# Stage 1 and the first projection of a three-stage layer in one written order, with scores on quarter tiles of TensorE

## The chip, the cores and the metric

The kernel runs on one core of one Trainium2 chip. The metric is the device time of one execution in microseconds (us). TensorE is called PE in the profile, VectorE DVE, ScalarE ACT, GpSimd POOL; SP issues the loads.

## What is computed

Three stages follow one another on a batch of 2 with 768 rows. The change touches the first stage and the first projection of the second.

```python
def _attn_ref(q, k, v):                       # 2 batches, 8 heads, 768 rows, 64 wide
    block, window = (32, 16)
    k_sum = k.reshape(B, H, nb, block, D).max(axis=3)      # 24 block keys
    v_sum = v.reshape(B, H, nb, block, D).mean(axis=3)     # 24 block values
    scores_l = scale * q @ k.T, masked to |i - j| < window
    scores_s = scale * q @ k_sum.T + log(block)
    a = softmax(concatenate([scores_l, scores_s], -1))
    return a @ concatenate([v, v_sum], 2)
def _moe_ref(x):       # 4 experts: q, k, v of 64 columns from x, causal softmax, @ v @ wo, top-2 gates
def _moe2_ref(x):      # token mixing (768 -> 256 -> 768), then channel mixing (512 -> 1536 -> 512)
```

## The kernel before, in words

Heads are taken in pairs, four to a batch. For each pair stage 1 cuts the 768 queries into 12 tiles of 64 rows, both heads of the pair stacked to 128 rows; the keys that a tile can see are a window of 96, and 24 block maxima stand behind them, 120 columns in all. Four tiles make a group (24 groups in the two batches, three to a pair).

A group goes through these steps, each named by a word in the list FIRST: S, scores on PE (`s1_scores`, L217; an f32 product takes two instructions; the query tile `qb` is spread over 128 rows with zeros for the other head, which is why `qb` is first set to zero, L634 and L635); mn, the masked minimum on DVE (`s1_minima`, L227); ex, the exps with their sums on ACT (L236); sm and ri, the inverse sums on POOL and DVE; mu, the products on POOL (L249 in batch 0, L252 in batch 1); T, four transposes on PE (L257); pT, their copy on ACT (L262); V, the product with the values on PE (L271), 64 columns at a time into one of two column halves; xh and xl, the high part by ACT (L279) and the low part by DVE (L282). Products later on are made of three terms of such high and low parts (`mm3`, L112 to L114).

Keys come as a ready window of 12 x 120 columns (`kwT`, tile `kx`), except for batch 0's first pair, which loads the plain keys (`kt`) and copies them into windows on DVE (L194 to L197). `km` (L185, L189) takes the block maxima and a copy (L187) puts them behind each window. Block means of v are made on PE in batch 0, by 12 products a pair with a matrix of zeros and 1/32 (`vm`, L293); in batch 1 by a DVE sum of a second copy of v (`vt`, L203) and a transpose (L208). POOL writes them behind the value windows (`vx`, L329, L211).

Batch 0's stage 1 stands in the written order FIRST: each engine is held to the order of the words. Batch 1's stage 1 (`s1`, one step a group) and the projection of batch 0 (`proj`, `pv` of 260 columns and `pj` of 384) are generators that `run` mixes by a share of progress, after which the planner of the framework orders the engines by its own estimate. `proj` copies q and k parts to their places by DMAs on the SP queue (L449 to L453). The SP queue issues in order: batch 0's loads, the projection weights, then batch 1's loads as the planner placed them, with the first token weights (`raw`, L140) among them. The score tiles have three PSUM banks (`sc`), transposes and block sums three (`pt`), values two (`acc`).

Of the kernel before, what the change touches and what calls it, by code (L numbers as in the profile page):

```python
# [39 lines left out]
kx0 S0 S1 mn0 ex0 S2 mn1 vm0.0 ex1 sm0 mn2 vm0.1 ri0 km1 mu0 vm0.2 ex2 kx1 sm1 T0 ri1 S3 mu1 pT0 S4  # L40
vme0 sm2 mn3 vx0 ex3 T1 ri2 mn4 S5 mu2 pT1 V0 mn5 ex4 sm3 vm1.0 ri3 km2 mu3 V1 xh0 T2 kx2 sm4 xh1 T3
xl0 ex5 vm1.1 ri4 xl1 mu4 vm1.2 pT2 sm5 S6 ri5 pT3 mu5 vme1 S7 mn6 vx1 ex6 T4 mn7 T5 S8 km3 ex7 sm6
V2 ri6 kx3 mu6 V3 mn8 xh2 S9 sm7 pT4 xl2 xh3 ri7 S10 pT5 mu7 mn9 ex8 T6 xl3 T7 V4 ex9 sm8 mn10 V5
wh0 S11 ri8 wh1 wl0 wh2 pT6 vm2.0 wl1 sm9 wh3 xh4 wl2 mu8 pT7 vm2.1 xl4 ex10 ri9 wl3 vm2.2 mn11 mu9
# [9 lines left out]
def stack_kernel(ctx: ExitStack, tc, qT, kT, kwT, vw, vT, wqkv, wo, tok1, tok2, ch1, ch2,  # L54
# [125 lines left out]

    def s1_keys(kt, vt, kx, vx):
        km = sp1.tile([P, NBLK], F32, name="km")
        sums = (kx[:, :, KW:KX], km[:, None, :].broadcast_to([P, NT, NBLK]))
        if kt is None:
            vec.tensor_reduce(km.rearrange("p (t n) -> p t n", t=NT),  # L185
                              kx[:, :, WIN:WIN + TQ].rearrange("p t (n c) -> p t n c", c=BLK), axis=AX.X, op=ALU.max)
            vec.tensor_copy(*sums)  # L187
# [12 lines left out]

    def s1_sums(kt, vt, kx, vx):
        vs = sp1.tile([P, NBLK], F32, name="vs")
        vec.tensor_reduce(vs, vt.rearrange("p (n c) -> p n c", c=BLK), axis=AX.X, op=ALU.add)  # L203
        return vs
# [586 lines left out]
```

## Time and profile before

| | us |
|---|---|
| median of 3 runs | 469.67 (468.07 to 472.20) |
| the profiled execution, whole | 467.73 |
| its span, from first to last instruction | 465.9 |
| PE, DVE, ACT, POOL busy | 445.1, 280.1, 231.2, 285.2 |

The rows below come from the one profiled execution, so sums are made against its 467.73 us. L numbers are lines of the kernel before; a line can be a helper's. Tile names in the rows are the program's, with numbers of buffers left out.

### The profile page before, as it was taken

Reading aid. Unit: us, or ns where it says so; the run is one execution under the profiler, and the core shown is the slowest. Engines: PE = TensorE matmul, PEld = TensorE weight load, DVE = VectorE, ACT = ScalarE, POOL = GpSimd, SP = SyncE. Lnnn points to the kernel's source line nnn. Section 1 sums busy time; section 2 is a strip of 40 time slices with the busy share of each in tenths; the row PEclk is TensorE's granted clock in tenths of the full one; section 3 lists DMA queues with packets and bytes.
Section 4 is the critical chain, followed back from the end, with each engine's and each line's share of the span. In section 5 each row is a group of like instructions: output and inputs, shape, how many; then the busy total and the mean of one; then the engine's idle time right before and its main releaser. Section 6 shows DMA issues by size and latency. Waiting matters only on the chain.

```text
span 465.9 us, 8565 instructions
## 1 busy us (share of the span) xinstructions
PE 445.1 (96%) x3038; PEld 420.7 (90%) x3038; DVE 280.1 (60%) x818; ACT 231.2 (50%) x653; POOL 285.2 (61%) x319
## 2 busy tenths in 40 slices
PE   7899899999989878999999999999999999999996
PEld 7798789989978766897999999999999999999996
DVE  5573766759699679868773743677572673332322
ACT  4685665977778687885664423233323321111010
POOL 4568542768989887997873869877864771000000
PEclk9999999999999999999999999999999999999999
DMA  7999917806515865021111120212121100001111
GB/s 222 275 255 310 289 39 207 182 2 167 127 46 152 210 171 146 3 91 45 45 47 46 66 70 2 84 53 78 58 91 45 62 32 0 1 0 69 68 70 68
DMA packets 28522, 46.51 MB, mean 100 GB/s; under 512 B 2496, under 2 KB 19648, under 8 KB 28480
## 3 DMA queue, kind: packets, MB, share of 16 engines
q1 hardware_dynamic: 28480, 45.97, 35.2%
q8 instruction: 24, 0.39, 0.4%
q14 instruction: 18, 0.15, 0.1%
HBM read 33.38 MB, written 3.15 MB: 78 GB/s over the span
## 4 chain that ended last, share of the span: by engine, by line
PE 68%; DMA 10%; DVE 7%; POOL 4%; ACT 3%; issue 3%; SPq 3%; DVEq 0%; ACTq 0%; POOLq 0%
PE h L113 7%; PE h L112 7%; PE h L114 7%; PE o L112 7%; PE o L113 7%; PE o L114 7%; DMA kx<-in_kwT_dram 5%; PE s1s L217 4%; PE s1a L271 2%; DMA qb<-in_qT_dram 2%; POOL pr L492 2%; PE u L112 2%; PE pj L112 2%; PE u L113 2%; PE u L114 2%
## 5 line engine op out<-in xcount | busy, mean ns | idle before, releaser
L144 POOL TENSOR_SCALAR deca<-deca 128x512 f32<-128x512 f32 x30 | 58.0, 1938 | 10.5 <-ACT deca L143 9.7
L113 PE MATMUL o<-hl,c2h 128*128 128x384 f32 x192 | 64.2, 337 | 0.0
L114 PE MATMUL o<-hh,c2l 128*128 128x384 f32 x192 | 64.0, 336 | 0.0
L108 ACT ACTIVATE hh<-h 128x384 fp32r<-128x384 f32 x48 | 23.3, 490 | 79.4 <-PE h L114 78.8
L109 DVE SCALAR_TENSOR_TENSOR hl<-h,hh 128x384 fp32r<-128x384 f32 x48 | 26.5, 555 | 53.2 <-ACT hh L108 53.2
L605 DVE TENSOR_TENSOR oa<-o,oa 128x384 f32<-128x384 f32 x64 | 31.9, 550 | 38.5 <-PE o L114 38.5
L112 PE MATMUL o<-hh,c2h 128*128 128x384 f32 x192 | 49.4, 336 | 0.0
L236 ACT ACTIVATE pr<-n,mn 128x120 f32<-128x120 f32 x96 | 36.6, 384 | 16.3 <-DVE mn L227 15.8
L150 POOL TENSOR_TENSOR raw<-raw 128x512 f32<-128x512 f32 x30 | 31.3, 1042 | 20.4 <-DVE raw L147 18.6
L492 POOL TENSOR_SCALAR pr<-pr,f,wg 128x128 f32<-128x128 f32 (+5 forms) x48 | 40.1, 849 | 5.1 <-DVE f L489 2.9
L151 POOL TENSOR_TENSOR deca<-deca,raw 128x512 f32<-128x512 f32 x30 | 40.8, 1360 | 1.0
L149 ACT ACTIVATE raw<-raw 128x512 f32<-128x512 uint32 x30 | 20.3, 677 | 36.3 <-DMA raw<-in_ch_dram 25.6
L145 DVE TENSOR_SCALAR deca<-deca 128x512 int32<-128x512 int32 x30 | 27.8, 928 | 14.9 <-POOL deca L144 14.9
L486 ACT ACTIVATE pr<-pr,mn 128x128 f32<-128x128 f32 (+5 forms) x48 | 31.9, 665 | 9.8 <-DVE mn L481 9.7
L113 PEld LDWEIGHTS o<-hl,c2h 128*128 128x128 f32 x192 | 36.0, 188 | 0.3 <-DVE hl L109 0.3
L114 PEld LDWEIGHTS o<-hh,c2l 128*128 128x128 f32 x192 | 36.0, 188 | 0.0
L112 PEld LDWEIGHTS o<-hh,c2h 128*128 128x128 f32 x192 | 34.8, 188 | 0.1
L113 PE MATMUL h<-u0l,c1h 128*128 128x384 f32 x96 | 32.5, 338 | 0.0
L112 PE MATMUL h<-u0h,c1h 128*128 128x384 f32 x96 | 32.4, 338 | 0.0
L114 PE MATMUL h<-u0h,c1l 128*128 128x384 f32 x96 | 32.3, 337 | 0.0
L112 PE MATMUL h<-u1h,c1h 128*128 128x384 f32 x96 | 32.3, 336 | 0.0
L113 PE MATMUL h<-u1l,c1h 128*128 128x384 f32 x96 | 32.3, 336 | 0.0
(207 smaller groups left out, 1315.1 us busy)
## 6 DMA issues: line engine op xcount, KB each, us to landing
raw<-in_ch_dram SPq DMA_DIRECT2D x24, 512.0 KB, 3.5
kx<-in_kwT_dram SPq DMA_DIRECT2D x7, 720.0 KB, 10.0
vx<-in_vw_dram SPq DMA_DIRECT2D x8, 576.0 KB, 11.1
qb<-in_qT_dram SPq DMA_DIRECT2D x16, 192.0 KB, 8.9
raw<-in_tok_dram SPq DMA_DIRECT2D x6, 512.0 KB, 4.6
out_dram<-oa SPq DMA_DIRECT2D x16, 192.0 KB, 2.0
vt<-in_vT_dram SPq DMA_DIRECT2D x4, 384.0 KB, 10.3
rqk<-in_wqkv_dram SPq DMA_DIRECT2D x4, 256.0 KB, 10.2
```

The lines of the kernel that those rows point to most:

```text
L109: vec.scalar_tensor_tensor(lo, src, 0.0, hi.bitcast(F32), op0=ALU.max, op1=ALU.subtract)
L112: ten.matmul(out, lh, rh, start=start, stop=False)
L113: ten.matmul(out, lh, rl, start=False, stop=False)
L114: ten.matmul(out, ll, rh, start=False, stop=stop)
L144: gps.tensor_scalar(af, af, F64_TINY, F64_HUGE, op0=ALU.max, op1=ALU.min)
L145: vec.tensor_scalar(ta, ta, 3, 0x3FFFFFFF, op0=ALU.logical_shift_left, op1=ALU.bitwise_and)
L150: gps.tensor_mul(lf, lf, ef)
L151: gps.tensor_add(af, af, lf)
L236: act.activation(pr[:, i, :], n[:, i, :], AF.Exp, bias=mn[:, i:i + 1], scale=-1.0, accum_out=sm[:, i:i + 1])
L486: act.activation(prs[r], prs[r], AF.Exp, bias=mn[:, r, ci:ci + 1], scale=-1.0, accum_out=sm[:, r:r + 1])
L492: gps.tensor_scalar(prs[r][:, :nk], prs[r][:, :nk], f[:, r:r + 1], wg[:, 3 * h + r, e:e + 1], op0=ALU.mult, op1=ALU.mult)
L605: vec.tensor_add(oa[d], a[:, :HALF], oa[d])
```

## The change

Both batches' stage 1 and the projection of batch 0 are now words of one written order (a for batch 0, b for batch 1, pv, vh, vl, pj, jh, jl and the gate's gA, gE, gB for the projection, whv0 and its like for weight splits, ld0 to ld3 for batch 1's loads). A score word u covers six tiles of a pair and writes two banks, one per head: each head and tile is a matmul of 64 rows by 64 columns of the array, at row half j and column half i % 2. Batch 0 reads the plain keys (800 columns) of every pair, loaded once, and makes 96 columns and 24 columns in two matmuls; batch 1 keeps windows of 120. Queries are loaded in one piece, without zeros. The minima, exps and products work on groups of three tile pairs (360 columns in place of 480). Batch 0's block sums of v go to four column tiles of 32, three products each; a DVE copy and one product (vs) add the four parts. Batch 0's xh is a DVE copy instead of an ACT copy. Batch 1's loads stand behind the score words that free their tiles; two of its query tiles lie in the buffers of the `raw` weights. `proj_parts` holds the steps of `proj` one by one; batch 1's projection runs through it as before.

```diff
+NU = NT // 4
+NSL = 2 * NT - 2 + 32
+KP = S + 2 * WIN
...
+akm0 aS0 amn0.0 aex0.0 amn0.1 aS1 ld0 aex0.1 avm0 amn1.0 amn1.1 aex1.0 asm0 ari0 apa0 amu0.0 akm1
+avs0 aex1.1 amu0.1 aT0.0 aS2 ame0 asm1 apT0.0 avx0 ari1 aT0.1 amn2.0 aex2.0 amn2.1 amu1.0 aS3 ld1
+amu1.1 apT0.1 aT1.0 aex2.1 amn3.0 aV0 amn3.1 aT1.1 apT1.0 axh0 asm2 avm1 apT1.1 axl0 aex3.0 aV1 ari2
+apa1 amu2.0 akm2 avs1 aex3.1 amu2.1 aT2.0 axh1 aS4 axl1 apT2.0 asm3 ari3 aT2.1 ame1 amn4.0 amu3.0
...
+bkm0 asm7 aV6 wlv3 ari7 bkc0 amu7.0 wlq1 bS0 axh6 amu7.1 aT7.0 axl6 whk1 apT7.0 aT7.1 bsu0 pv0 whk2
+apT7.1 whk3 wlk1 whq2 bmn0.0 bvs0 whq3 bex0.0 aV7 wlq2 wlq3 bS1 axh7 wlk3 vh0 axl7 pv1 bme0 bmn0.1
+bvx0 bex0.1 bkm1 pv2 vh1 bkc1 bsm0 bri0 vl1 bmu0.0 pv3 vh2 wlk2 bmu0.1 vl2 bT0.0 vh3 pv4 vl0 bpT0.0
...
+bT3.0 bxh2 bT3.1 bpT3.0 bS4 bxl2 bpT3.1 bvs3 jh2 bmn4.0 bV3 bme3 bmn4.1 bex4.0 bvx3 pj4 jl2 bxh3
+bex4.1 bxl3 bS5 jh3 bsm4 pj5 bmn5.0 jh4 bex5.0 bmn5.1 bri4 jl3 bmu4.1 bex5.1 jl4 bS6 bmu4.0 pj6 jh5
+bmn6.0 bex6.0 bmn6.1 bsm5 bri5 jl5 bmu5.0 bex6.1 pj7 bmu5.1 jh6 jl6 bsm6 bT4.0 bri6 jh7 bT4.1 bmu6.0
+bS7 bpT4.0 jl7 bpT4.1 bmu6.1 bT5.0 bmn7.0 bT5.1 bex7.0 bT6.0 bmn7.1 bV4 bex7.1 bxh4 bsm7 bri7 bpT5.0
+bxl4 bmu7.0 bpT5.1 bT6.1 bpT6.0 bV5 bmu7.1 bpT6.1 bT7.0 bxh5 bV6 bpT7.0 bxl5 bT7.1 bxh6 bpT7.1 bxl6
+bV7 bxh7 bxl7
 """
...
     def s1_load(b, hp, qb):
-        first = b == 0 and hp == 0
-        kx = unit([P, NT, KX], F32, f"kx{b}{hp}")
-        kt = None
-        if first:
-
-            kt = kt0
-            vec.memset(kx[:, 0, KW:KX], 0.0)
-
+        kx = unit([P, KP + NBLK] if b == 0 else [P, NT, KX], F32, f"kx{b}{hp}")
         vt = half([P, S], F32, "vt") if b else None
         vx = unit([P, NT, P], F32, f"vx{b}{hp}")
-        loads = [(kt, kT) if first else (kx, kwT[b, hp])]
-        loads += [(qb[i::2, :, i, :], qT[b, hp, i::2].rearrange("p (t c) -> p t c", c=P)) for i in range(2)]
-        if first:
+        loads = [(kx, kwT[hp]) if b else (kx[:, :KP], kT[hp]), (qb, qT[b, hp])]
+        if b == 0 and hp == 0:
             loads += [(lmask, lmask_d), (ident, ident_d), (blocks, blocks_d)]
-        loads += ([(vt, vT[b, hp])] if b else []) + [(vx[:KW], vw[b, hp])]
+        loads += ([(vt, vT[hp])] if b else []) + [(vx[:KW], vw[b, hp])]
         for d, src in loads:
-            if b == 0:
-                r = tc.keep_in_program_order(nc.sync.dma_start(d, src))
-            else:
-                with tc.issue_after(last["load"].ins):
-                    r = nc.sync.dma_start(d, src)
-        last["load"] = r
-        return kt, vt, kx, vx
-
-    def s1_keys(kt, vt, kx, vx):
-        km = sp1.tile([P, NBLK], F32, name="km")
-        sums = (kx[:, :, KW:KX], km[:, None, :].broadcast_to([P, NT, NBLK]))
-        if kt is None:
+            tc.keep_in_program_order(nc.sync.dma_start(d, src))
+        return kx, vt, vx
...
+    class Stage1:
...
+        def km(self, hp):
+            kx = self.lds[hp][0]
+            if self.b == 0:
+                vec.tensor_reduce(kx[:, KP:], kx[:, WIN:WIN + S].rearrange("p (n c) -> p n c", c=BLK), axis=AX.X, op=ALU.max)
+                return
+            km = self.box["km", hp] = sp1.tile([P, NBLK], F32, name="km")
...
+        def kc(self, hp):
+            vec.tensor_copy(self.lds[hp][0][:, :, KW:KX], self.box["km", hp][:, None, :].broadcast_to([P, NT, NBLK]))
...
+        def vm(self, hp):
+            pv = self.box["vm", hp] = bank("pt", f"vm{self.b}{hp}")
+            for t in range(NT):
+                c = 32 * (t % 4)
+                ten.matmul(pv[c:c + 32, P:2 * P], blocks[:KW, 2 * (NT - 1 - t):2 * (NT - 1 - t) + 32],
+                           self.lds[hp][2][:KW, t, :], start=t < 4, stop=t >= NT - 4)
...
+        def pa(self, hp):
+            parts = self.box["pa", hp] = sp1.tile([P, P], F32, name="parts", bufs=1)
+            vec.tensor_copy(parts, self.box["vm", hp][:, P:2 * P])
...
+        def vs(self, hp):
+            if self.b == 0:
+                ten.matmul(self.box["vm", hp][:NBLK, :P], blocks[:, NSL:], self.box["pa", hp], start=True, stop=True)
+                return
+            pv = self.box["vm", hp] = bank("pt", f"vm{self.b}{hp}")
+            ten.transpose(pv[:NBLK, :P], self.box["su", hp], ident)
...
+        def S(self, u):
+            qb, kx = self.qbs[u // 2], self.lds[u // 2][0]
+            sc = self.box["S", u] = [bank("sc", f"s1s{self.b}{u}{j}") for j in range(2)]
+            for part in range(1 if self.b else 2):
+                for i in range(6):
+                    t = 6 * (u % 2) + i
+                    for j in range(2):
+                        hs = slice(64 * j, 64 * j + 64)
+                        c = KX * (i // 2)
+                        if self.b:
+                            cs, k = slice(c, c + KX), kx[hs, t, :]
+                        elif part == 0:
+                            cs, k = slice(c, c + KW), kx[hs, TQ * t:TQ * t + KW]
+                        else:
+                            cs, k = slice(c + KW, c + KX), kx[hs, KP:]
+                        ten.matmul(sc[j][64 * (i % 2):64 * (i % 2) + 64, cs], qb[hs, TQ * t:TQ * t + TQ], k,
+                                   start=True, stop=True)
...
+        def mn(self, u, j):
+            n = sp1.tile([P, NU, KX], F32, name="n", bufs=3)
+            mn = sp1.tile([P, NU], F32, name="mn", bufs=6)
+            for i in range(NU):
+                t = NU * (u % 2) + i
+                mi = 0 if t == 0 else (2 if t == ST - 1 else 1)
+                vec.tensor_tensor_reduce(n[:, i, :], self.box["S", u][j][:, KX * i:KX * i + KX], lmask[:, mi, :],
+                                         scale=-0.125, scalar=BIG, op0=ALU.add, op1=ALU.min, accum_out=mn[:, i:i + 1])
+            self.box["mn", u, j] = n, mn
...
+        def xh(self, u):
+            hi, av = self.out(u, 0), self.box["V", u][:, :HALF]
+            last["x"] = vec.tensor_copy(hi, av) if self.b == 0 else act.activation(hi, av, AF.Copy)
...
-    def s1(xh, xl, qbs):
...
+    def proj_parts(b, xs, out, tags):
+        q2, k2, k2l, V = [], [], [], []
         out.extend((q2, k2, k2l, V))
-        lg = gp.tile([P, ST, NE], F32, name="lg", bufs=1)
-        for st in range(ST):
-            a = bank(next(rr), f"pv{b}{st}")
+        gate = {}
...
+        return dict(pv=pv, vh=vh, vl=vl, gA=gA, gE=gE, gB=gB, pj=pj, jh=jh, jl=jl)
...
-    qbs = []
-    for i in range(HP):
-        qb = sp1.tile([P, ST, 2, P], F32, name="qb", bufs=2) if i < 2 else unit([P, ST, 2, P], F32, f"qb{i}")
-        (vec if i < 2 else gps).memset(qb[:, :3], 0.0)
-        gps.memset(qb[:, 3:], 0.0)
-        qbs.append(qb)
+    qbs = [sp1.tile([P, S], F32, name="qb", bufs=2) for i in range(2)]
+    q0s = qbs + [half([P, S], F32, f"qb{i}") for i in range(2, HP)]
...
-    def w_split():
-        for w, r in zip(wqk, raws[1:]):
-            for k in range(HP):
-                with tc.issue_after(last["mul"].ins):
-                    split_h(w[0][:, k], r[:, k])
-                    with tc.issue_after(last["mn", 0, HP - 1, 2].ins):
-                        split_l(w[0][:, k], w[1][:, k], r[:, k], gps if k == HP - 1 else vec)
-                yield
...
+    first = Stage1(0, q0s)
     for hp in range(HP):
-        lds.append(s1_load(0, hp, qbs[hp]))
+        first.ld(hp)
...
+    second = Stage1(1, qbs + [dec.tile([P, S], F32, tag="raw", name=f"qd{i}") for i in range(2)])
     sts = [[], []]
-    g1 = s1(*xs[1], qbs[:2])
-    p0 = proj(0, *xs[0], sts[0])
-    run((12, g1), (18, part(p0, 10)), (2 * HP, w_split(), 0, 0.3))
+    p0 = proj_parts(0, first.halves, sts[0], rot(("acc", "pt", "sc")))
+    ws1 = {w: (t, r) for w, t, r in zip("vqk", (wv, *wqk), raws)}
+
+    def step(word):
+        stem = word.rstrip("0123456789.")
+        num = [int(x) for x in word[len(stem):].split(".") if x]
+        if word[:2] in ("wh", "wl"):
+            (w, r), k = ws1[word[2]], num[0]
+            if word[1] == "h":
+                split_h(w[0][:, k], r[:, k])
+            else:
+                split_l(w[0][:, k], w[1][:, k], r[:, k], gps if k == HP - 1 else vec)
+        elif stem == "ld":
+            second.ld(*num)
+        elif stem in p0:
+            p0[stem](*num)
+        else:
+            getattr((first, second)["ab".index(stem[0])], stem[1:])(*num)
+
+    in_order(FIRST.split(), step)
...
-    run((4, p0, 0, 0.2), (16, attn(0, *sts[0], yTs[0])), (14, proj(1, *xs[1], sts[1]), 0, 0.9), (8, wt_load(), 0.4, 0.8))
+    run((16, attn(0, *sts[0], yTs[0])), (14, proj(1, *xs[1], sts[1]), 0, 0.9), (8, wt_load(), 0.4, 0.8))
```

## Rows read from the trace of the kernel before

**Rows 1.** The first part of the page: busy us, share of the span, instructions.

```profile
PE 445.1 (96%) x3038; PEld 420.7 (90%) x3038; DVE 280.1 (60%) x818; ACT 231.2 (50%) x653; POOL 285.2 (61%) x319
```

**Rows 2.** Busy time by stretch: engines, then granted clock, DMA share, GB/s.

```profile
6.70:101.50 94.80, 88.22 (x946) 80.31 (x944) 57.30 (x312) 65.52 (x275) 53.69 (x111) 1.00 0.78 206
6.70:60.00 53.30, 47.67 (x524) 43.34 (x523) 30.85 (x173) 35.29 (x154) 32.80 (x59) 1.00 1.04 278
...
120.00:200.00 80.00, 72.26 (x447) 61.84 (x446) 67.13 (x197) 61.42 (x159) 71.60 (x74) 1.00 0.44 114
```

**Rows 3.** TensorE in order of time: start, us, line, operation, tiles, [idle before].

```profile
6.74 2.98 PE L217 MATMUL s1s<-kx,qb 128*128 128x120 f32 x24
...
15.93 2.12 PE L217 MATMUL s1s<-kx,qb 128*128 128x120 f32 x16 [1.20 <-DMA qb<-in_qT_dram]
...
111.45 0.33 PE L114 MATMUL pj<-x0h,wqk1l 128*128 128x384 f32 x1
```

**Rows 4.** The same view: neighbours from which distances of starts are read.

```profile
22.74 1.93 PE L293 MATMUL vm<-vx,blocks 96*24 96x128 f32 x16
...
75.51 1.09 PE L217 MATMUL s1s<-kx,qb 128*128 128x120 f32 x8
76.44 0.60 PE L257 MATMUL s1p<-ident,pr 128*120 128x128 f32 x4
76.97 0.69 PE L271 MATMUL s1a<-pTs,vx 120*64 120x64 f32 x16
77.58 0.45 PE L112 MATMUL pj<-x0h,wqk0h 128*128 128x384 f32 x1
77.87 0.34 PE L113 MATMUL pj<-x0l,wqk0h 128*128 128x384 f32 x1
78.04 0.34 PE L114 MATMUL pj<-x0h,wqk0l 128*128 128x384 f32 x1
```

**Rows 5.** TensorE groups, 0 to 112 us: count | busy, mean ns | idle before.

```profile
L217 PE MATMUL s1s<-kx,qb 128*128 128x120 f32 x192 | 27.3, 285 | 4.9 <-DVE mn L227 3.6 <-DMA qb<-in_qT_dram 1.2
L257 PE MATMUL s1p<-ident,pr 128*120 128x128 f32 x96 | 16.4, 277 | 0.0
L271 PE MATMUL s1a<-pTs,vx 120*64 120x64 f32 x384 | 15.7, 227 | 0.0
L293 PE MATMUL vm<-vx,blocks 96*24 96x128 f32 x96 | 11.4, 273 | 1.7 <-DMA vx<-in_vw_dram 1.7
```

**Rows 6.** Waits, 0 to 112 us, engines and SP queue: total, times, longest.

```profile
DVE km L185 <- DMA kx<-in_kwT_dram: 13.5, 5, 5.8
...
SPq L449 <- ACT s000h L104: 18.3, 1, 18.3
```

**Rows 7.** The SP queue in order of time: start, us, what it issued.

```profile
0.72 0.39 SPq L174 DMA_DIRECT2D kt<-in_kT_dram  x1
1.88 1.43 SPq L174 DMA_DIRECT2D qb<-in_qT_dram  x2
...
32.28 1.53 SPq L177 DMA_DIRECT2D kx<-in_kwT_dram  x1
...
74.45 0.79 SPq L177 DMA_DIRECT2D kx<-in_kwT_dram  x1
```

**Rows 8.** ACT and DVE groups, 0 to 112 us.

```profile
L279 ACT ACTIVATE x0h<-s1a 128x256 fp32r<-128x256 f32 x12 | 4.2, 368 | 0.2 <-PE s1a L271 0.2
...
L227 DVE CUSTOM_DVE_ANT_0 n<-s1s,lmask 128x120 f32<-128x120 f32 x96 | 21.4, 277 | 7.3 <-PE s1s L217 5.7 <-ACT pTs L262 1.0 <-ACT pr L236 0.5
...
L105 DVE TENSOR_TENSOR V<-pv,V 128x128 fp32r<-128x128 f32 x18 | 4.9, 283 | 2.3 <-ACT V L104 2.1
...
L105 DVE TENSOR_TENSOR s010l<-pj,s010h 128x384 fp32r<-128x384 f32 x2 | 1.1, 554 | 0.0
```

**Rows 9.** Load issues of the run: count, KB each, us to landing.

```profile
kx<-in_kwT_dram SPq DMA_DIRECT2D x7, 720.0 KB, 10.0
...
kt<-in_kT_dram SPq DMA_DIRECT2D x1, 400.0 KB, 2.9
```

More of the change, by code (lines that the diff above doesn't have):

```diff
@@ L39 @@
 FIRST = """
[L40 to L44, printed above, removed]
@@ new lines, in ri, with mu @@
+        def ri(self, u):
+            ri = self.box["ri", u] = sp1.tile([P, 2, NU], F32, name="ri", bufs=4)
+            vec.reciprocal(ri, self.box["sm", u])
+        def mu(self, u, j):
+            pr, ri = self.box["ex", u, j], self.box["ri", u]
+            if self.b == 0:
+                gps.tensor_mul(pr, pr, ri[:, j, :, None].broadcast_to([P, NU, KX]))
+                return
+            for i in range(NU):
+                gps.tensor_scalar(pr[:, i, :], pr[:, i, :], ri[:, j, i:i + 1], 1.0, op0=ALU.mult, op1=ALU.mult)
@@ new lines, in T, with pT, V @@
+        def T(self, u, j):
+            pT = self.box["T", u, j] = bank("pt", f"s1p{self.b}{u}{j}")
+            for i in range(NU):
+                ten.transpose(pT[:KX, P * i:P * i + P], self.box["ex", u, j][:, i, :], ident)
+        def pT(self, u, j):
+            pTs = self.box["pT", u, j] = sp1.tile([P, HALF], F32, name="pTs", bufs=4)
+            act.activation(pTs[:KX], self.box["T", u, j][:KX, :HALF], AF.Copy)
+        def V(self, u):
+            av = self.box["V", u] = bank("acc", f"s1a{self.b}{u}")
+            for i in range(6):
+                cs = slice(64 * i, 64 * i + 64)
+                for j in range(2):
+                    sl = slice(64 * j, 64 * j + 64)
+                    ten.matmul(av[sl, cs], self.lds[u // 2][2][:KX, 6 * (u % 2) + i, sl], self.box["pT", u, j][:KX, cs],
+                               start=True, stop=True)
@@ L336, in s1_first, with halves, in_order @@
+        def halves(self):
+            return [self.x[i][0] for i in range(2)], [self.x[i][1] for i in range(2)]
+    def in_order(words, steps):
         traced = nc.cur_bb.bb.instructions
-        for word in FIRST.split():
+        for word in words:
             at = len(traced)
-            op = word.rstrip("0123456789.")
-            if op == "vm":
-                block(*map(int, word[2:].split(".")))
-            elif op != "km":
-                step(op, int(word[len(op):]))
+            steps(word)
@@ L401, in proj, with words, vh @@
                     kt == 0, kt == HP - 1)
+        def words(st, i):
+            return [V[i][:, st, :, 64 * c:64 * c + 64] for c in range(2)], \
+                gate["pv", st][:, P * i:P * i + P].rearrange("p (e c) -> p e c", e=2)
+        def vh(st):
             for i in range(2):
[L403 to L406 removed]
@@ new lines, in pj @@
+        def pj(n):
+            p, c0, h = n // 4, n // 2 % 2, n % 2
+            if n % 4 == 0:
+                for t, x in ((q2, "q2"), (k2, "k2"), (k2l, "k2l")):
+                    t.append(unit([P, 2, S], F32R, f"{x}{b}{p}"))
+            xh, xl = xs()
+            a = gate["pj", n] = bank(next(tags), f"pj{b}{c0}{p}{h}")
+            x = slice(HALF * h, HALF * h + HALF)
+            for kt in range(HP):
+                i, j = kt // 2, kt % 2
+                mm3(a[:, :HALF], wqk[p][0][:, kt, c0, :], wqk[p][1][:, kt, c0, :], xh[i][:, j, x], xl[i][:, j, x],
+                    kt == 0, kt == HP - 1)
@@ L764 @@
         key = TQ * t + c
-        lmask[:, i, :KW] = np.where(band & ((key >= 0) & (key < S))[None, :], 0.0, NEGB)
+        rows = (slice(0, 64), slice(0, P), slice(64, P))[i]
+        lmask[:, i, :KW] = np.where(band, 0.0, NEGB)
+        lmask[rows, i, :KW] = np.where(band & ((key >= 0) & (key < S))[None, :], 0.0, NEGB)[rows]
     cmask = np.zeros((P, 512), np.float32)
     cmask[:, 512 - P:] = np.where(np.triu(np.ones((P, P), bool), 1), NEGB, 0.0)
-    blocks = np.zeros((KW, 2 * NBLK - 2), np.float32)
+    blocks = np.zeros((P, NSL + NBLK), np.float32)
+    for i in range(4):
+        blocks[32 * i:32 * i + NBLK, NSL:] = np.eye(NBLK)
     for i in range(2):
```

351 lines of the change are left out of this document (119 added, 232 removed).

## The prediction

> **What bounds the kernel now.** I read the page's first part, then the busy time by stretch, then TensorE's groups and its order of time in the first 112 us, then what its gaps and the load queue waited for. TensorE (PE) carries the kernel: 96% of the span [rows 1], always at the full 2.4 GHz level (granted clock 1.00 in every stretch of [rows 2]). The change touches the part until batch 0's last projection matmul starts at 111.45 us [rows 3]. From 6.7 to 101.5 us PE is busy 88.2 of 94.8 us, ACT 65.5, DVE 57.3, POOL 53.7, and the 16 DMA engines are full only until 60 us (share 1.04, 278 GB/s) [rows 2]. So PE is first, with loads second while they last. What the change is worth is PE time removed plus PE gaps removed, less new gaps.
>
> A row's duration is no price on PE, since neighbours overlap (a score instruction lasts 285 ns, its successor starts long before). The price is the distance of starts [rows 4]: 8 score instructions from 75.51 to 76.44 us, 116 ns each; 16 instructions of the value product from 76.97 to 77.58, 38 ns each. An f32 product is two instructions.
>
> PE's gaps after 6.74 us, by the groups' idle column [rows 5]: scores 4.9 us (3.6 behind DVE's minima, 1.2 behind a load), block sums 1.7 behind a load; 6.6 in all. The minima were late because DVE stood 13.5 us on loads of `kx` [rows 6]. These loads are late by themselves: batch 1's first is issued at 32.28 us, and its last only at 74.45 us, since the SP queue stood 18.3 us behind a `q` copy that waited for `s000h` [rows 6, 7].
>
> **Part by part.** *Scores.* Before: 192 instructions at 116 ns, 22.3 us. After: a matmul per head and tile on a quarter of the array. Batch 1 has 192 instructions of 120 columns; batch 0 has 192 of 96 columns and, since its keys are no longer copied into windows, 192 more of 24. No row shows tiles that differ in rows. The value product shows two column tiles: 64 columns take 38 ns per instruction, and the two passes that make 120 columns take 116 would take 62 for 64 columns, so two do run side by side [rows 4]. Bounds: four side by side, in proportion to columns, 29 + 23 + 6 ns, 192 each: 11.2 us. None side by side: 116 + 93 + 38 ns, 47.4 us. Two: 58 + 47 + 38 ns, 27.5 us. I take 29 ns for 120 columns, the same for 96 (I expect no better pace than that), and the value product's 38 ns for the 24, its nearest row: 192 x 96 ns = 18.4 us. Gain 3.9 us.
>
> The page "TensorE: Matmul & The Clock Gate" of the Trainium skill (Back-to-back issue gap) gives a floor of about 25 ns between starts however few the columns, which speaks against the 24-column pieces: by it they cost 4.8 us rather than my 7.3, and never the 1.2 of my lower bound. No run here shows it.
>
> *Block sums of v, batch 0.* Before 96 instructions of 128 columns [rows 5], 16 from 22.74 in 1.93 us, some 117 ns each [rows 4]: 11.2 us. After, 96 of them on four column tiles in turn: 28 ns if four wide, 117 if alone; I take the 38 ns of the product that already runs on column tiles, 3.6 us. Added are four sums over the four parts, two instructions each at 117 ns, 0.9 us, and a DVE copy of 128x128 for each (0.28 us by the V words [rows 8], covered, DVE being 60% busy). Gain 6.7 us.
>
> *Changes of tiling.* After the value product the next projection matmul takes 0.29 us to its successor instead of 0.17, and four transposes before it take 0.53 instead of 0.44 [rows 4]: 0.1 us for a change. The written list has 63 of them on PE. Before, the scores made none; the values came in 24 words (now 16) and the block sums in about twelve visits (now eight), by my count in the code under 50 changes. So 10 to 15 more; cost 1.0 to 1.5 us, I take 1.0, since before's list also breaks up words.
>
> The page "TensorEngine Tiling (Array Packing)" of the Trainium skill (Key Properties) says that a change of tiling mode drains the engine, which speaks against this change: see the third rival. The rows above show a change at 0.1 us, well short of an instruction's whole length.
>
> *Loads.* Batch 0's keys are 400 KB for each of three pairs in place of 720 [rows 7, 9]: 960 KB less, 3.5 us at 278 GB/s. Six memsets of `qb` on POOL and two on DVE go, of which the first query load waited for two (issue at 1.88 us [rows 7]); queries take one issue each instead of two. All batch 1 loads are issued right behind the scores that free their tiles, ahead of any `q` or `k` copy, so the 18.3 us wait has nothing left to hold up. The second pair's queries land at 15.93 us before [rows 3]; 320 KB less (1.2 us) and the earlier start (1.1) make it about 13.6. Until then PE has two score words (2 x 1.6), sums 1.1 and transposes 0.4: 4.7 of 6.9 us, gap 2.2. The later gaps behind minima (3.6) ended on loads; of these I take 1.8, because a written order keeps PE waiting in line where a planner might have found other work. Gaps 4.0 in place of 6.6: gain 2.6 us. Bounds: 0.0 and 10 us of gaps.
>
> *Off the path.* Minima and transposes keep their counts (96 each, and the exps with them), values keep 384 instructions [rows 5, 8], the projection all of its own. ACT hands batch 0's `xh` (12 x 0.37 us) to DVE (8 copies, 0.55 us by the 128x384 subtraction) and pays about 1.6 us for 32 transposed copies in place of 24; DVE loses four window copies of keys and two memsets; POOL's products lie in 16 calls instead of 12 at the same elements [rows 8]. No engine passes PE's total. Two score banks per word out of three make the next word wait for a minima word of 0.7 us; PE has transposes and values to run there.
>
> Sum against the profiled 467.73 us (span 465.9): 3.9 + 6.7 - 1.0 + 2.6 = 12.2, giving 455.5. The median of the runs shown is 469.67, 1.9 higher; the same gain gives 457.5. What is late next is PE itself: projection and tails, then attention as before.
>
> **The rivals.**
> 1. *Row tiles do not run side by side* (slower). Scores cost 47.4 instead of 18.4 us: 457.5 + 29 = 486.5. For it: no row shows row tiles. Against: the value product's column tiles do overlap. It ends slower once the 576 score instructions cost over 30.6 us, 53 ns each on average. Chance 0.07. If only two overlap, 27.5 us: 466.6, no change by the measurement; 0.10.
> 2. *The gain is given back in attention.* In 120 to 200 us POOL is busy 71.6 of 80 and PE 72.3 [rows 2]; if POOL's chain (weights of the token stage, whose raw tiles now hold queries until the last score words) sets that stage's end, work in front is free: 467 to 470. Against: POOL has slack until 101.5 and moves forward with the rest. Chance 0.12.
> 3. *A change of tiling costs a full drain*, 285 less 116 ns by the score row, 0.17 us. 63 changes cost 10.7 instead of 6.3: 461.9. Chance 0.06. This is the skill's rule; the rows have it at 0.1.
> 4. *The written order stalls PE*: one late word (a bank, a load, a POOL product) holds all behind it. With 10 us of gaps more than I allow: 468, with 16 slower than 474. Chance 0.08, half of it slower.
> Forecast: 0.57, 449 to 463 (four-wide scores at 11.2 give 450.3).
>
> **How the numbers follow.** A measurement of this kernel tells 1%, 4.7 us, from no change. Faster by more: forecast 0.57, rival 3 0.06, a share of rivals 1 and 2 that ends just under 465, 0.05: 0.68. Within 1%: two-wide 0.07, rival 2 0.10, half of rival 4 0.04: 0.21. Slower: 0.07 + 0.04 = 0.11. The range reaches from four-wide scores and no gaps, 448, to the same-time cases, 469.
>
> **What would show it.** Right: 24 score instructions of batch 1 in 0.7 us and 48 of batch 0 in 1.5; 24 block-sum instructions in 0.9 us; DVE's wait for `kx` loads near zero; batch 1's last key load issued by 50 us; batch 0's last projection matmul and batch 1's last value product 10 to 12 us of PE work earlier; PE's gaps in the first stage near 4 us; 120 to 200 us shifted, not stretched. Wrong: score starts 80 ns apart or more, PE idle behind POOL or banks, or an attention stage longer by what the first stage lost.

## The result, and the profile after

The changed kernel takes 475.44 us (474.63 to 475.79, 4 runs) where the kernel before, beside it, takes 469.23 (468.07 to 472.2, 4 runs): ratio 1.0145, 95% interval 1.0111 to 1.0178. It is slower by about 6 us, where 457.5 and at most 469 had been forecast. The profiled run of the change took 475.79 us, with a span of 474.0. Of two kernels tried further down, late_k and own_ch_first, the execution that was profiled was about 1% slower than most of that kernel's others, so those two profiles are not read.

First the page's parts 1 to 3 of the kernel after: busy us, share and instructions of the engines, TensorE (PE) first, the granted clock in 40 slices, and one of the two queues that carry instructions. The clock and the queue of the kernel before stand below them.

```profile
PE 443.4 (94%) x3430; PEld 411.9 (87%) x3430; DVE 277.0 (58%) x800; ACT 226.6 (48%) x645; POOL 276.9 (58%) x309
...
PEclk9897999888999989899999999999999999999999
...
q8 instruction: 27, 0.44, 0.4%
```

```profile
PEclk9999999999999999999999999999999999999999
...
q8 instruction: 24, 0.39, 0.4%
```

PE is busy as long as before [rows 1], but the clock row has slices of 7 and 8, which the kernel before had nowhere. The view by windows says where, in this order: stretch, its length, busy us of PE, PEld, DVE, ACT, POOL, granted clock, DMA share, GB/s.

```profile
16.00:20.00 4.00, 4.00 (x68) 3.15 (x72) 2.27 (x14) 1.25 (x6) 0.33 (x2) 0.57 1.02 300
33.00:41.00 8.00, 5.83 (x70) 4.19 (x69) 2.54 (x16) 2.64 (x10) 4.47 (x9) 0.57 1.03 298
91.00:99.00 8.00, 6.21 (x46) 5.54 (x45) 3.96 (x23) 5.34 (x22) 3.57 (x11) 0.57 0.96 211
115.00:119.00 4.00, 4.00 (x19) 3.57 (x19) 2.01 (x10) 2.09 (x8) 3.13 (x4) 0.57 0.45 131
173.00:177.00 4.00, 3.42 (x12) 3.02 (x13) 3.20 (x11) 1.37 (x4) 2.79 (x4) 0.57 1.00 239
190.00:194.00 4.00, 3.92 (x14) 2.94 (x14) 2.11 (x7) 2.34 (x7) 3.83 (x5) 0.57 0.14 31
```

A mean of 0.57 in 4 us is 3.4 us at the 1.2 GHz level and the rest at 2.4; the six rows hold 27.3 us at 1.2 GHz, which does at most 13.7 us of full-speed work. Next, the same view by stage; the first, third and fourth row answer to [rows 2], the second reaches to the last `u` product of the token stage, the last is the place that the second group of experiments turns on.

```profile
6.70:101.50 94.80, 82.92 (x1302) 70.45 (x1302) 60.39 (x303) 60.85 (x263) 53.09 (x107) 0.91 0.80 216
101.50:287.60 186.10, 173.51 (x1062) 155.22 (x1061) 129.22 (x353) 120.82 (x300) 143.29 (x139) 0.97 0.28 78
...
6.70:60.00 53.30, 44.94 (x881) 36.59 (x881) 37.18 (x190) 34.19 (x155) 31.31 (x52) 0.90 0.96 275
...
120.00:200.00 80.00, 69.91 (x402) 58.81 (x402) 58.41 (x179) 58.78 (x152) 67.52 (x74) 0.96 0.44 113
...
165.00:205.00 40.00, 30.82 (x164) 23.47 (x163) 27.92 (x78) 28.28 (x73) 28.95 (x32) 0.91 0.43 111
```

In 165 to 205 us the kernel before, read in the same way, does 219 matmuls at full clock; its last `u` product comes at 279.85 us, in the change at 287.43:

```profile
101.50:280.00 178.50, 169.18 (x1029) 153.25 (x1028) 132.78 (x352) 120.76 (x296) 146.16 (x138) 1.00 0.34 94
...
165.00:205.00 40.00, 35.54 (x219) 29.73 (x218) 33.03 (x93) 32.24 (x83) 35.77 (x36) 1.00 0.38 105
```

The products themselves became cheap. TensorE in order of time, kernel after (start, us, line, operation, tiles, count, [idle before]):

```profile
24.48 0.86 PE L211 MATMUL vm<-vx,blocks 96*32 96x128 f32 x24
25.27 1.04 PE L252 MATMUL s1s<-kx,qb 64*64 64x96 f32 x48
26.24 0.54 PE L293 MATMUL s1p<-ident,pr 128*120 128x128 f32 x3
26.71 0.40 PE L224 MATMUL vm<-parts,blocks 128*24 128x128 f32 x2
...
28.75 1.04 PE L252 MATMUL s1s<-kx,qb 64*64 64x96 f32 x48
29.72 0.92 PE L305 MATMUL s1a<-pTs,vx 120*64 120x64 f32 x24
30.57 1.07 PE L252 MATMUL s1s<-kx,qb 64*64 64x96 f32 x37
35.17 0.62 PE L252 MATMUL s1s<-kx,qb 64*64 64x24 f32 x11 [3.52 <-issue]
...
60.83 0.85 PE L252 MATMUL s1s<-kx,qb 64*64 64x120 f32 x24
61.61 0.28 PE L227 MATMUL vm<-ident,vs 128*24 128x128 f32 x1
```

By distances of starts a score word of batch 0 takes 0.97 us (28.75 to 29.72), one of batch 1 0.78 (60.83 to 61.61), and the block sums of a pair 0.79 (24.48 to 25.27). Against [rows 4] the four quarter tiles do run side by side. The row at 35.17 shows what came in: a stop of 3.52 us in the middle of a score word, "issue", with no releaser. PE's groups and DVE's waits, 0 to 112 us, answer to [rows 5, 6]:

```profile
L252 PE MATMUL s1s<-kx,qb 64*64 64x96 f32 (+2 forms) x480 | 13.5, 240 | 6.2 <-issue 5.0 <-DVE mn L261 0.7 <-DVE kx L205 0.4
L293 PE MATMUL s1p<-ident,pr 128*120 128x128 f32 x96 | 17.9, 314 | 4.2 <-POOL pr L288 1.8 <-ACT pTs L297 1.7 <-POOL pr L285 0.5
...
DVE s011l L424 <- DMA k2l<-s001l: 7.4, 1, 7.4
...
DVE kx L198 <- DMA kx<-in_kT_dram: 2.7, 1, 2.7
```

DVE's 13.5 us on key loads fell to 2.7, the wait for the first load ahead of PE's start, nearly as forecast. But a new wait of 7.4 us stands there: the fourth q/k word needs a buffer that the copies of the second still read. Behind it in line on DVE stood an inverse sum that POOL's products and the transposes need, which is 1.8 of the 4.2 us of the second row, and batch 1's last minima. ACT stood 4.0 us at the same word's high part, with the copies of the transposes behind it: another 1.7.

### The profile page after: what moved, and what is told of

Same layout as the page of the kernel before. It is cut to its first block, busy times and chain, and to the rows that moved or that the text cites. A ratio compares the mean times of both kernels' runs of the same rounds, so it can differ in the third digit from the quotient of the medians.

```text
span 474.0 us, 9305 instructions
## 1 busy us (share of the span) xinstructions
PE 443.4 (94%) x3430; PEld 411.9 (87%) x3430; DVE 277.0 (58%) x800; ACT 226.6 (48%) x645; POOL 276.9 (58%) x309
## 5 line engine op out<-in xcount | busy, mean ns | idle before, releaser
L168 POOL TENSOR_TENSOR raw<-raw 128x512 f32<-128x512 f32 x30 | 31.6, 1053 | 24.1 <-DVE raw L165 18.8
L486 POOL TENSOR_SCALAR pr<-pr,f,wg 128x128 f32<-128x128 f32 (+5 forms) x48 | 37.6, 794 | 4.5 <-DVE f L483 4.0
L163 DVE TENSOR_SCALAR deca<-deca 128x512 int32<-128x512 int32 x30 | 25.3, 843 | 15.3 <-POOL deca L162 15.2
```

Of the source, the lines that this page charges most:

```text
L163: vec.tensor_scalar(ta, ta, 3, 0x3FFFFFFF, op0=ALU.logical_shift_left, op1=ALU.bitwise_and)
L168: gps.tensor_mul(lf, lf, ef)
L486: gps.tensor_scalar(prs[r][:, :nk], prs[r][:, :nk], f[:, r:r + 1], wg[:, 3 * h + r, e:e + 1], op0=ALU.mult, op1=ALU.mult)
```

## The experiments

All times are compared with runs of the kernel before on the same chip; the rows come from several chips, so from row to row ratios are compared and not medians. "Half clock" is the time at 1.2 GHz in the profiled run, added up from windows of 1 us to 260 us; the kernel before has none there in its profiled run. It is one execution each, and it varies from one to the next: by their mean clocks (0.968 to 0.975) the four runs of the kernel after all lost about as much, and 86 further runs of the kernel before have mean clocks of 0.985 to 1.000, where the profiled one has 0.998.

| run | median us | ratio to before, 95% | half clock us |
|---|---|---|---|
| after | 475.44 | 1.0145 (1.0111 to 1.0178) | 27.3 |
| own_s011 | 473.92 | 1.0148 (1.0064 to 1.0233) | 23.9 |
| late_ld | 475.24 | 1.0175 (1.0118 to 1.0232) | 27.3 |
| fill_tail | 473.52 | 1.0116 (1.0055 to 1.0176) | 17.1 |
| late_k | 473.08 | 1.0093 (1.0054 to 1.0132) | not read |
| ch_first | 471.93 | 1.0092 (1.0050 to 1.0135) | 17.0 |
| own_ch_first | 467.25 | 0.9976 (0.9944 to 1.0008) | not read |
| both_again | 470.11 | 1.0018 (0.9971 to 1.0064) | 23.9 |
| own_ch_first_fl | 470.94 | 1.0057 (1.0019 to 1.0096) | 17.1 |
| before_ch_last | 469.78 | 1.0060 (1.0028 to 1.0091) | 6.8 |
| both_merge | 466.01 | 0.9955 (0.9926 to 0.9984) | 20.5 |
| both_late_ld | 467.35 | 0.9975 (0.9936 to 1.0013) | 13.7 |
| both_merge_late_ld | 465.65 | 0.9941 (0.9914 to 0.9967) | 17.1 |
| after_merge | 470.59 | 1.0047 (1.0011 to 1.0084) | 23.9 |
| best_fill | 463.90 | 0.9850 (0.9776 to 0.9924) | 10.2 |

### The waits of the first stage

*own_s011*: the fourth q/k word's high and low part get a buffer of their own.

```diff
-                gate["s", n // 2] = [half([P, S], F32R, f"s{b}{p}{c0}{x}") for x in "hl"]
+                gate["s", n // 2] = ([half([P, S], F32R, f"s{b}{p}{c0}{x}") for x in "hl"] if b or n // 2 < 3 else
+                                     (lambda t: [t[:, i] for i in range(2)])(unit([P, 2, S], F32R, "s011")))
```

> The two tiles of the last projected keys (s011) get a buffer of their own instead of waiting for the copies out of s001. Theory A (the forecast gain was lost in waits that let TensorE's clock fall): DVE's 7.4 us wait for k2l<-s001l at 84 us is gone, the clock stays at 1.00 from 85 to 105 us, batch 1's last value product ends near 98 instead of 105 us, and the time is 468 to 470 us against 475.4. Theory B (the gain is given back in attention, whose end is set by other engines): the first stage ends 5 to 7 us earlier, but the time stays within 2 us of 475.4.

*late_ld*: batch 1's loads are issued later.

```diff
-aS1 ld0 ... aS3 ld1 ... aS5 ld2 ... aS7 ld3
+aS5 ld0 ... aV4 ld1 ... aV7 ld2 ... pv5 ld3
```

> Batch 1's four groups of loads are issued later (behind aS5, aV4, aV7, pv5), so that less is queued on the DMA engines at 31 us. Theory A, second part (PE's 3.5 us gap at 31.6 us, which no instruction released, is code that has to come through the loaded DMA engines): that gap falls below 1 us, the clock stays at 1.00 from 33 to 40 us, batch 0's values end 4 to 6 us earlier, time 470 to 472. If the gap is something in the written order: it stays, 475. Theory B: 475 whatever the gap does. If the loads now come too late: DVE or PE wait for kx or vx of batch 1, over 477.

*fill_tail*: four idle products ahead of batch 1's transposes (word `fl0` ahead of `bT5.0`).

```diff
+        elif stem == "fl":
+            a = bank("sc", f"fl{num[0]}")
+            for i in range(4):
+                ten.matmul(a, ident, cmask, start=True, stop=True)
```

> Four more products of 128x512 (eight instructions of about 0.43 us, 3.4 us in all; their result is not used) stand on PE in front of the transposes bT5 that wait. The DVE wait stays. If the half clock after the wait is what costs: clock 1.00 from 91 to 98 us, the transposes and values behind the wait run at full pace, 472 to 474. If the clock costs nothing there (another engine sets the end): 475 to 476. If PE's own work sets the end: up to 479.

*late_k*: the last two projection words with their copies move behind transposes of batch 1.

```diff
-bmu4.0 pj6 jh5 ... bex6.1 pj7 bmu5.1 jh6 jl6 ... bri6 jh7 bT4.1 ... bpT4.0 jl7
+bT5.1 pj6 jh6 jl6 ... bT6.1 pj7 jh7 jl7
```

> The last two projection products and their splits (pj6, pj7 with jh and jl) stand behind bT5.1 and bT6.1 instead of ahead of bT4, nothing else is changed. Theory A: the DVE wait is shorter than 3 us and comes behind the last minima, PE has 4 us of products to run in the tail, no fall of the clock at 91 us, 468 to 471. Theory B: 475. If the later k copies hold up attention instead: 475 or more, with s2s waiting for k at 100 us.

All four moved the time by 2.4 us or less. In own_s011 the wait of 7.4 us and ACT's of 4.0 are gone and the last value product of stage 1 ended at 96.97 us instead of 105.06, yet the time hardly fell. Of the 8.1 us, 6.1 are still there at 168 us, product against same product; at the attention's last one 2.7 are left (245.03 after 247.69). Most of what was given back went in one place, as the same window shows for own_s011:

```profile
165.00:205.00 40.00, 30.37 (x150) 26.26 (x151) 26.55 (x71) 23.73 (x60) 27.98 (x28) 0.79 0.26 75
```

150 matmuls in 40 us, at a mean clock of 0.79. So something there holds what comes earlier. late_ld shows a second thing. TensorE in order of time, and two windows of it:

```profile
20.64 0.55 PE L251 MATMUL s1s<-kx,qb 64*64 64x96 f32 x13
23.07 1.45 PE L251 MATMUL s1s<-kx,qb 64*64 64x96 f32 x35 [1.88 <-issue]
```

```profile
22.00:23.00 1.00, 0.00 (x0) 0.00 (x0) 0.00 (x0) 0.00 (x0) 1.00 (x2) 1.00 1.10 286
23.00:24.00 1.00, 0.93 (x31) 0.93 (x32) 0.00 (x0) 0.00 (x0) 0.91 (x2) 0.57 1.16 299
```

The word stops after 13 of its 48 instructions, where after stops too (13 at 22.22, 0.44 us), DVE and ACT run dry, and the clock falls. The stop of 3.52 us is gone in this run, as its theory A expected, but this one of 1.88 stands ahead of it, and the time is 475.24, not 470 to 472. The DMA engines were still full here (share 1.10).

### Where the attention stood

From here on, theory A is that the gain is lost where ACT stands, in its written order, at the decode of channel weights; B, that the attention is merely ordered otherwise. SP's queue, ACT and TensorE of the kernel after, each in order of time:

```profile
166.09 0.46 SPq L429 DMA_DIRECT2D k<-s111h  x1
...
170.79 1.41 SPq L433 DMA_DIRECT2D k2l<-s111l  x2
172.29 2.02 SPq L158 DMA_DIRECT2D raw<-in_ch_dram  x2
```

```profile
179.07 0.66 ACT L161 ACTIVATE deca<-raw 128x512 f32<-128x512 f32 x1 [2.61 <-DMA raw<-in_ch_dram]
```

```profile
180.70 0.44 PE L506 MATMUL s2a<-ph,V 128*128 128x384 f32 x1 [1.71 <-ACT ph L122]
...
198.00 0.45 PE L506 MATMUL s2a<-ph,V 128*128 128x384 f32 x1 [2.17 <-ACT ph L122]
```

In the kernel before the same queue has the weights first:

```profile
163.45 2.17 SPq L140 DMA_DIRECT2D raw<-in_ch_dram  x2
169.29 0.47 SPq L449 DMA_DIRECT2D k<-s111h  x1
```

After the change they are issued behind eight copies of k, in a stretch where the DMA engines are full (share 1.00 from 173 to 177); they land at 179. ACT has them next in line and waits 2.61 us, with the `ph` copies of the attention behind it, and PE waits for `ph`.

*ch_first*: only that order is turned round. `decode_load` is the load of `decode_w` by itself; the eight copies are issued behind it.

```diff
+            if b == 1 and n == 7:
+                for j in range(2):
+                    ahead.append(decode_load(ch1[:, P * j:P * j + P].rearrange("(k p) n -> p k n", p=P), 512))
...
+                        if b == 1 and n == 7:
+                            with tc.issue_after(ahead[-1][1].ins):
+                                nc.sync.dma_start(d.bitcast(F32), src.bitcast(F32))
```

> The kernel after, with the first two loads of channel weights issued ahead of the last eight copies of k rather than behind them, and nothing else. Theory A (the front's gain is lost where ACT, in its written order, stands at the decode of those weights: 2.6 us at 179 and 2.5 us at 196, with the attention's copies queued behind it and TensorE at half clock for 6.8 us after its gaps): both waits go, half clock between 165 and 200 goes from 6.8 us to at most 3.4, the last attention product comes 3 to 7 us earlier than 247.7, and the time is 468 to 472. Theory B (what is lost in the attention is the same work in another order on all engines, whatever the loads do): the two waits go but the end moves by under 2 us, 474 to 476.

*own_ch_first* has the edits of own_s011 and ch_first; *both_again* is the same kernel in the next batch of runs.

> The same, with the last pair of q/k words in a buffer of their own as well (in which the first stage's 7.4 us wait was gone and batch 1's first part was done 9 us sooner). Theory A: the two faults add up, the front's 9 us now reach the end of the attention, which comes at 235 to 239, time 462 to 467, under the kernel before. Theory B: the attention still ends at 243 to 246, time 472 to 475.

> The kernel with the two edits (own buffer for the last pair of words, channel weights loaded ahead of the last copies of k) once more, as the base of the three runs beside it and for its trace. Theory A: no half clock and no wait of ACT over 1.5 us between 165 and 205, 465 to 468. What is left of the half clock lies ahead of 60 us, after stops in which TensorE waits for nothing that the profile shows.

*own_ch_first_fl* adds the idle products of fill_tail to them.

> The same, with four idle products of 512 columns on TensorE where it had waited at the end of the first stage, to hold its clock. If the half clock counts by itself: 1 to 2 us under the run with the two edits alone (3.4 us less at half clock is worth about 1.7). If only the waits count: the same within 0.7 us.

*before_ch_last* is the kernel before with its weight loads held behind the last copy of k.

```diff
-            decode_w(*(x[:, j, :].rearrange("p (k n) -> p k n", k=HP) for x in t[:2]), ch1[:, P * m:P * m + P].rearrange("(k p) n -> p k n", p=P), 512)
+            with tc.issue_after(last["k"].ins):
+                decode_w(*(x[:, j, :].rearrange("p (k n) -> p k n", k=HP) for x in t[:2]), ch1[:, P * m:P * m + P].rearrange("(k p) n -> p k n", p=P), 512)
```

> The reverse in the kernel before: its channel-weight loads, two of which stood ahead of the last copies of k, are held behind them, as in the kernel after. Theory A: ACT then waits 2 to 4 us at the first decode, TensorE's clock falls once or twice between 165 and 205 (it never did), and the time goes up by 3 to 6 us, to 470 to 473 where the kernel before is at 467. Theory B: within 1 us of the kernel before.

ch_first: the loads are issued at 162.74 us, ACT's wait is 0.76 us at 167.80 instead of 2.61 at 179.07, and the window runs at full clock with 211 matmuls instead of 164:

```profile
165.00:205.00 40.00, 34.86 (x211) 27.92 (x210) 32.75 (x86) 32.17 (x81) 31.29 (x32) 1.00 0.37 103
```

The attention's last product comes 5.1 us earlier (242.62). The ratio falls from 1.0145 to 1.0092, some 2.5 us: A's direction, but the two intervals overlap, so by itself it shows little. With the own buffer as well it is 0.9976 and 1.0018 in two batches, level with the kernel before. The buffer, worth nothing that can be measured alone, is now worth 3.5 to 5.4 us (0.0074 to 0.0116), and the order of the loads, beside own_s011 (1.0148), 6 to 8 (0.0130 to 0.0172); both are clear of the noise. That is what A says and B does not. The first of the two missed its 462 to 467 by little; the second, at 470.11, missed 465 to 468 by more. Its attention ended at 242.18, where 235 to 239 had been expected, so only part of what the front gained came through. It had 3.4 us of half clock at 169 us, no wait of ACT over 1.1 us in the window, and 4.8 us of stops in the score words with 13.6 us of half clock ahead of 45 us. The reverse agrees: in before_ch_last ACT waits 2.6 us and the time rises by 0.6% (2.8 us, expected 3 to 6):

```profile
ACT deca L143 <- DMA raw<-in_ch_dram: 2.6, 1, 2.6
```

The idle products of own_ch_first_fl missed: 0.4 to 0.8% slower than the same kernel without them. Where the wait that they had filled is gone, they are probably work on the path, which no run shows by itself; in fill_tail, with the wait, they cost nothing that can be measured.

### The stops in the score words

Four stops of the kernel after lie on PE between 14 and 36 us without a releaser (1.03, 0.44, 0.17 and 3.52 us). In the view of DMA traffic, cut at the longest one (31.6 to 35.2 us): queue, kind, packets, MB, share. The first row is from 31.6 to 32.6, the next two from 32.6 to 33.7, the last from 33.7 to 35.1.

```profile
q1 hardware_dynamic: 126, 0.38, 99.1%
```

```profile
q1 hardware_dynamic: 81, 0.34, 107.2%
q8 instruction: 1, 0.02, 5.7%
```

```profile
q1 hardware_dynamic: 67, 0.32, 99.4%
```

One packet of instructions (16 KB, by 0.44 MB in 27) passes in the stop, through engines that loads fill, and PE goes on at 35.17, some 1.5 us behind it or more. The other three stops fit. In the trace of after, packets of this queue end at 14.41, 21.71, 26.65 and 33.67 us, and PE goes on at 15.93, 23.21, 28.13 and 35.17, 1.5 us behind each. The queue also follows PE's count: 24 packets for 3038 matmul instructions before, 26 for 3334 in after_merge, 27 for 3430 in after. Theory: PE's own instructions come late. Its test is fewer of them.

*both_merge*: own_ch_first, with batch 0's products with the 24 block maxima made for two tiles at once. *after_merge*: the kernel after with this alone.

```diff
+                    if part and i % 2:
+                        continue
                     for j in range(2):
                         hs = slice(64 * j, 64 * j + 64)
                         c = KX * (i // 2)
+                        if part:
+                            ten.matmul(sc[j][:, c + KW:c + KX], qb[hs, TQ * t:TQ * t + P], kx[hs, KP:], start=True, stop=True)
+                            continue
```

> The two edits, and batch 0's products of scores with the block maxima in pairs of tiles: 6 of 128 columns of q in a word where there were 12 of 64, so 48 products fewer by 45 us. If TensorE's stops in the score words are its own instructions arriving late through loaded DMA engines: the second stop moves by some words and the sum of the stops falls by 1 us or more, with 3 us or more of half clock: 463 to 466. If the stops are something else (a tiling change, a wait that the trace lacks): they stand at the same words, and only the products' 0.1 us a word is gained: 466 to 467.

> The kernel after with the paired block-maxima products alone. If the stops in the score words are instructions coming late: no stop over 1 us that waits for nothing, 471 to 474. If they went only because the runs before had other loads or a lower clock at that time: stops of 1 to 3.5 us stay and the time is 474 to 476.

*both_late_ld* and *both_merge_late_ld* are own_ch_first and both_merge with the later loads of late_ld.

> The two edits, and batch 1's four loads issued two to five units later, so that the DMA engines are less loaded from 20 to 45 us. If instructions late through loaded DMA engines make the stops: the longest stop goes from 2 to 3 us down to 2 or less and the time is 464 to 466. If not: 466 to 469, with batch 1's keys awaited at the end of the first stage.

> Both of the last two edits over the base. Late instructions: the stops together under 2 us, half clock ahead of 60 us at most 6.8, 462 to 465, under the kernel before. Otherwise 466 to 469.

PE's score groups from 6.7 to 45 us, of after and then of after_merge:

```profile
L252 PE MATMUL s1s<-kx,qb 64*64 64x24 f32 (+1 forms) x384 | 10.1, 233 | 5.8 <-issue 5.0 <-DVE mn L261 0.7
```

```profile
L257 PE MATMUL s1s<-kx,qb 64*64 64x96 f32 (+1 forms) x212 | 8.1, 280 | 0.9 <-DVE mn L266 0.6 <-DVE kx L205 0.4
L249 PE MATMUL s1s<-kx,qb 64*128 64x24 f32 x96 | 8.1, 299 | 0.0
```

The 5.0 us of stops are gone, with 96 matmul instructions fewer, and the ratio falls from 1.0145 to 1.0047, 4.6 us (expected 471 to 474, got 470.59). In both_merge they are gone too, ratio 0.9955; there the pairs are worth less, 1.0 us beside own_ch_first, which is within the noise, and 3.0 beside both_again. The stops differ from profile to profile, but not on this point: in the eight read that lack the pairs they come to 2.8 to 7.5 us, in the four that have them to none. A lower clock is no excuse: from 26 to 40 us both_merge ran at 2.4 GHz without a stop. The later loads by themselves did not help: in both_late_ld the stops are as long (6.5 us, longest 3.5), so it is the smaller count of instructions that ends them, not the later loads. On top of the pairs they change nothing that can be measured (0.9955 to 0.9941), and 465.65 is just above what was expected. What missed in both kernels with the pairs is the clock: 13.6 us at half clock stand there without a stop, from 11 or 12 us on.

### The clock of the first 30 us

*best_fill*: both_merge_late_ld, with idle products of 128 columns in the waits at 8 to 12 us (`fl2` behind `aS0`, `fl3` behind `avm0`, `fl1` behind `avs0`).

```diff
+        elif stem == "fl":
+            for i in range(num[0]):
+                ten.matmul(spare[:, :P], idle, idle, start=True, stop=True)
```

> The kernel with all four edits (own buffer, channel weights ahead, paired block-maxima products, batch 1's loads later) and six idle products of 128 columns where TensorE waits for VectorE between 8 and 12 us. If its clock falls at 12 us because of those short waits: the 13.6 us at half clock between 12 and 26 are gone or at most 6.8, and the time is 460 to 464. If something else makes it fall: the half clock stays and the time is 465 to 467.

TensorE of best_fill in order of time, and its first stage by windows beside that of both_merge_late_ld, without the idle products:

```profile
8.07 0.71 PE L685 MATMUL spare<-idle 128*128 128x128 f32 x4
8.71 1.02 PE L264 MATMUL s1s<-kx,qb 64*64 64x96 f32 x24
...
11.24 0.94 PE L685 MATMUL spare<-idle 128*128 128x128 f32 x6
```

```profile
6.70:60.00 53.30, 51.41 (x862) 43.27 (x862) 42.92 (x211) 37.83 (x173) 35.22 (x60) 0.97 0.96 276
```

```profile
6.70:60.00 53.30, 48.54 (x775) 39.90 (x767) 38.81 (x189) 34.16 (x154) 31.62 (x52) 0.87 0.99 269
```

The half clock from 12 to 27 us is gone, 87 matmuls more are done by 60 us (12 of them idle), and the ratio falls from 0.9941 to 0.9850: 463.9 us, the best of all and under both kernels. It is not the profiled run alone: its four runs have mean clocks of 0.987 to 0.996, the ten without the idle products 0.973 to 0.983. So it was the short waits of PE there that had let the clock fall: 0.57, 0.67 and 0.40 us between 8 and 12 us in both_merge_late_ld. How dear that can be is hinted at by best_fill's own runs: 460.06 us at a mean clock of 0.996, 463.96 and 463.83 at 0.987; 0.009 of 462 us is 4.2, and 3.8 is the difference. But this is one run at the higher clock, and the fourth took 467.39 at the same 0.987.

## Why the prediction was wrong

*Scores: right, and under-sized.* 8 words of 0.97 us and 8 of 0.78 are 14.0 us, where I had 18.4 and the bounds 11.2 to 47.4; gain 8.3 instead of 3.9. Row tiles do run side by side, so rival 1 fell, its two-wide case too. The 24-column products were most of the error: a batch 0 word of 96 and 24 columns takes 20 ns an instruction, 0.97 us over 48. The page "TensorE: Matmul & The Clock Gate" of the Trainium skill (Back-to-back issue gap) has some 25 ns as the least; the measurement decides, and it is less on quarter tiles.

*Block sums: right.* 3.2 us and, for the sums of the parts, some 0.33 each (two instructions): 4.5 in all, as forecast.

*Changes of tiling: priced too low.* Three transposes between two changes take 0.47 us from start to start (26.24 to 26.71), where 0.11 each, the pace of [rows 4], gives 0.33: the end of one change and the beginning of the other, some 0.14 for a whole one and not 0.1. From 6.7 us until the last `u` product (279.85 us before, 287.43 after) PE is busy 257.4 us before (88.22 [rows 2] and 169.18) and 256.4 after (82.92 and 173.51), of which some 24 at half clock (27.3 less some 3 idle), so some 244 at full speed: 13.2 less. Scores and sums would give 15.0; that leaves 1.8 for the changes, where 1.0 had been taken. Rival 3 did not fall by this. Its 0.17 is nearer to the 0.14 than my 0.1, and its 4 us came of charging all 63 changes with the difference, though the nearly 50 of the kernel before would pay it too. The page "TensorEngine Tiling (Array Packing)" of the Trainium skill (Key Properties) says that a change of mode drains the engine; no run here tells a drain from 0.14 us.

*Loads: right.* Batch 1's last keys are issued at 41.25 us (74.45 before [rows 7]), DVE's wait for keys is 2.7 (13.5 before [rows 6]).

*The step that failed is "Gaps 4.0 in place of 6.6: gain 2.6".* Batch 1's last value product, forecast 10 to 12 us earlier, came 3.5 later (105.06 us, 101.54 before). PE is idle 11.9 us from 6.7 to 101.5 (94.8 less 82.92) in place of 6.6. Of these, 5.2 are the stops for instructions, for which I had no row and no term: I had priced the 576 score instructions by PE's time alone. 3.5 more are waits at 88 to 93 us: 1.8 behind the DVE wait of 7.4 and 1.7 behind ACT's of 4.0, both for one buffer, since both go when the word gets its own (own_s011). That is rival 4's mechanism (one late word holds all).

*The second that failed stands unspoken in "then attention as before".* The clock. I took 1.00 from [rows 2] for the kernel after as well, and it had 27.3 us at half clock, which costs up to 13.7. And the loads of the channel weights moved behind the copies of k. Rival 2 (the gain is given back in attention) had the place right and named the `raw` tiles, but for the weights of the token stage and by POOL's chain; it was ACT's line, at the channel weights. Why the planner put them there is read from the code alone: the decodes ahead of them come later. Idle time from 6.7 us to the last `u` rose from 15.9 to 24.5 us.

The sum by these measures: 13.2 us less work at full speed, some 12.2 more by the clock, 8.6 more idle: 7.6 later at the last `u`, as it is (287.43 less 279.85). It closes by its making, since the 13.2 is what busy time and half clock leave; the 15.0 by distances of starts is the independent measure. The saving was real and larger than forecast (9.6 for scores, sums and changes); it was paid out again by four faults, each of which an experiment above takes away: the weight loads' place 2.5 us, and with it the buffer 3.5 to 5.4, the instructions 4.6 (1.0 to 3.0 with the first two gone), the clock of the first 30 us 4.3 (0.9941 to 0.9850). What is left open: why the kernel before kept its full clock in its profiled run through waits of 1.7 and 1.2 us [rows 3, 5], when shorter ones lowered it here. The products around the waits differ too (the whole array there, quarter tiles here), and no run separates the two; by the mean clocks most other runs of the kernel before did lose some microseconds. The loads' share in the late instructions is inferred from the DMA view; a front with idle DMA engines was not tried.

## To carry to other kernels

Cutting a product into many short ones is paid in instructions as well as in TensorE's time: count them, and look for stops without a releaser where the DMA engines are full. A gain in front is worth only what the next shared queue lets through, so compare the order of that queue (here SP's, weights against copies) in both kernels before counting on "the rest as before". And a shorter stage with the same small waits can lose its clock: read the granted clock first, and try idle products in waits that can't be removed, but not on the path.

## What the runs showed of the hardware

- Four quarter tiles of 64 by 64 run side by side: 32 ns an instruction for 120 columns (0.78 us over 24), 116 for the whole array before.
- Stops of PE of up to 3.5 us without a releaser while the DMA engines are full; each of the four in after ends 1.5 us behind a 16 KB packet of the instruction queue. With 96 matmul instructions fewer there is none.
- A change of tiling costs some 0.14 us between starts (three transposes between two changes: 0.47 us instead of 0.33).
- The clock stood at 1.2 GHz for 13.6 us between 12 and 27 us behind waits of 0.57, 0.67 and 0.40 us (both_merge_late_ld); with 12 short idle instructions in them it stayed at 2.4 there (best_fill).
